# Cutting the last two output tiles of a two-layer MLP by columns, side by side, instead of tile by tile

## The chip, the cores and the metric

The kernel runs on one core of a Trainium2 chip. The metric is the device time of one execution in microseconds. The profile counts from the core's first profiled instruction; its span is about 1.3 us shorter than the timed figure. All timed comparisons below use executions in the fast state, and the granted TensorE clock in them (the share of full speed that the chip allowed) is 1.0. A store's landing is the last of the semaphore updates by which the DMA engines report it done.

## The reference

```python
# x: 2048 x 448, w1: 448 x 1792, w2: 1792 x 448, all bfloat16
h = jnp.einsum("bsd,df->bsf", x, w1) + b1
h = jax.nn.gelu(h, approximate=True)
return jnp.einsum("bsf,fd->bsd", h, w2) + b2
```

## The kernel before

The 2048 rows are worked through in four chunks of 512, that is four output tiles of 128 rows each. Layer 1 leaves gelu(h), transposed, in `g`: 14 blocks of 128 features. Layer 2 contracts over those 14 blocks. Each block is split into its lower and upper 64 rows, and the two halves of the TensorE array work on them side by side. I call them the two lanes. A "unit" is a pair of PSUM banks. In pass "a" the lower lane writes bank 0 and the upper lane bank 1; in pass "b" they swap, so that each bank has seen all 128 rows.

```python
def part(self, name, fts):                      # one pass of a unit
    for ft in fts:                              # 14 feature blocks: 14 "steps"
        for lo in (0, 1):                       # bank
            half = lo if name == "a" else 1 - lo    # lane
            rows = slice(half * H, (half + 1) * H)
            o = 0
            for i, (tile, d0, n) in enumerate(self.banks[lo]):
                # ... one matmul of n columns, with a weight load of its own
                mm(u, lo, half, slice(o, o + n), g[rows, ft, j * P:(j + 1) * P],
                   w2_sb[rows, ft, d0:d0 + n], ...)
                o += n
    # after pass "b": drain. Bank 0 by VectorE (adds b2), in the last chunk's q and r
    # bank 1 by ScalarE (copies; b2 is already in it, by a matmul of ones with b2)
```

The last chunk cannot hide its own drains and stores, so it is cut to leave little for the end. With tile numbers within the chunk, columns from and count (DQ = 112):

```python
p = Layer2(c, [(0, 0, D)], [(1, 0, D)])                          # tiles 0 and 1, 448 columns each
q = Layer2(c, [(2, 0, 3 * DQ)], [(2, 3 * DQ, DQ), (3, 0, 2 * DQ)])
r = Layer2(c, [(3, 2 * DQ, DQ)], [(3, 3 * DQ, DQ)])
p.part("a", every); q.bias(1); r.bias(0); q.part("a", every)
p.part("b", every); r.part("a", every)
q.part("b", every); r.part("b", every)
# ... stores of tiles 0 and 1, then:
store(j + 2, [("o", j + 2, 0), ("o", j + 2, 3 * DQ)])            # SP, 128 rows of 896 bytes
store(j + 3, [("o", j + 3, 0)], 0, 2 * DQ)                       # SP, 128 rows of 448 bytes
store(j + 3, [("o", j + 3, 2 * DQ), ("o", j + 3, 3 * DQ)], 2 * DQ, D, "scalar")
```

## Time and profile before

| | before |
|---|---|
| median time, three runs at first | 93.97 us |
| median time, six runs beside the changed kernel | 94.12 us (93.96 to 94.34) |
| span of the profiled run | 92.8 us |
| matmuls | 969 |
| first bias matmul of the last chunk | 82.263 us |
| start of VectorE's last drain | 90.656 us |
| issue of the last store (ScalarE) | 91.027 us |
| its first packet | 92.007 us |
| its last landing | 92.777 us |

The lower rows are read from the records behind the timeline and the DMA packets, to three decimals. The first bias matmul is a good zero, because everything that the change touches in the last chunk lies after it.

### The profile page before, as it was taken

The numbers are of one execution on the slowest core, as the hardware profiler recorded it, in microseconds if no ns is written. First come the engines' busy times: TensorE is split into PE (matmuls) and PEld (weight loads), VectorE is DVE, ScalarE is ACT, GpSimd is POOL, SyncE is SP. The second block draws the span as 40 slices with busy tenths as digits, with TensorE's granted clock in tenths as the row PEclk, the third lists the DMA queues.
The fourth block names the chain that finished last, engine by engine and source line by source line (L and its number), as shares of the span: only waits on it lengthen the run. The fifth ranks groups of instructions, "written<-read, shape, count | busy, mean of one in ns | idle before, by whom it ended". The sixth has DMA issues, their size and how long they took to land.

```text
span 92.8 us, 2119 instructions
## 1 busy us (share of the span) xinstructions
PE 89.8 (97%) x969; PEld 47.9 (52%) x969; DVE 13.9 (15%) x38; ACT 38.2 (41%) x64; POOL 1.7 (2%) x8
## 2 busy tenths in 40 slices
PE   6999999999999999999999999999999999999990
PEld 2455444555554444555544444555554444579990
DVE  0176000210442000000433000000333000000331
ACT  6033978600004787800003787900002888900021
POOL 6000000000000000000000000000000000000000
PEclk9999999999999999999999999999999999999999
DMA  2999994955747000000033000000022000000023
GB/s 46 342 273 337 375 297 43 207 96 112 70 90 221 14 0 7 0 0 0 0 103 102 0 0 4 0 7 0 0 99 99 7 0 0 0 0 7 0 99 99
DMA packets 12888, 7.32 MB, mean 79 GB/s; under 512 B 7248, under 2 KB 12688, under 8 KB 12880
## 3 DMA queue, kind: packets, MB, share of 16 engines
q1 hardware_dynamic: 11904, 6.75, 31.3%
q10 hardware_dynamic: 944, 0.45, 1.6%
q8 instruction: 7, 0.11, 0.5%
q14 instruction: 1, 0.01, 0.0%
q0 software_dynamic: 32, 0.00, 0.0%
HBM read 3.79 MB, written 1.84 MB: 61 GB/s over the span
## 4 chain that ended last, share of the span: by engine, by line
PE 97%; ACT 0%; issue 0%
PE u L221 92%; PE u L196 4%; PE u L358 1%; ACT out_sb L338 0%
## 5 line engine op out<-in xcount | busy, mean ns | idle before, releaser
L279 ACT ACTIVATE g<-u,b_f 128x512 bf16<-128x512 f32 x56 | 34.8, 685 | 39.5 <-PE u L221 39.5
L221 PE MATMUL u<-w_sb,g 64*128 64x448 bf16 (+3 forms) x532 | 43.3, 320 | 0.0
L221 PE MATMUL u<-xT,w_sb 64*128 64x512 bf16 (+1 forms) x342 | 41.3, 375 | 0.1
L221 PEld LDWEIGHTS u<-w_sb,g 64*128 64x128 bf16 x532 | 25.9, 94 | 16.9
L221 PEld LDWEIGHTS u<-xT,w_sb 64*128 64x128 bf16 x342 | 17.0, 94 | 19.1 <-DVE xT L371 0.3
L341 DVE TENSOR_TENSOR out_sb<-u,b_bc 128x448 bf16<-128x448 f32 (+2 forms) x16 | 8.9, 590 | 62.5 <-PE u L221 62.5
L221 PE MATMUL u<-xT,w1r 64*128 64x512 bf16 x56 | 10.5, 376 | 0.0
L221 PEld LDWEIGHTS u<-xT,w1r 64*128 64x128 bf16 x56 | 2.8, 94 | 3.2
L338 ACT CAST out_sb<-u 128x112 bf16<-128x112 f32 (+1 forms) x3 | 0.8, 286 | 8.8 <-PE u L221 8.8
L196 PE MATMUL u<-const-bfloat16-1.0 128*128 128x512 bf16 (+1 forms) x8 | 3.4, 601 | 0.8 <-PEq L498 0.8
L369 ACT COPY xT<-u 64x256 bf16<-64x256 bf16 (+1 forms) x3 | 1.1, 369 | 3.7 <-PE u L358 2.3
L196 PEld LDWEIGHTS u<-const-bfloat16-1.0 128*128 128x128 bf16 x8 | 1.0, 139 | 2.4 <-issue 2.4
L371 DVE TENSOR_SCALAR xT<-u 128x128 uint32<-128x128 uint32 (+1 forms) x7 | 1.8, 288 | 0.8 <-PE u L358 0.8
L179 ACT ACT_TABLE_LOAD x1 | 1.3, 1283 | 0.8 <-PEq L498 0.8
L449 DVE COPY b_z<-b_bc 1x112 bf16<-1x112 bf16 (+1 forms) x3 | 0.5, 188 | 7.0 <-DMA b_bc<-in_b_dram 6.9
L358 PEld LDWEIGHTS u<-ident,xn 64*128 64x128 bf16 x24 | 0.9, 127 | 0.7 <-issue 0.7
L191 DVE COPY xT<-xT 64x512 bf16<-64x512 bf16 x3 | 0.9, 289 | 2.0 <-DMA xT<-in_x_dram 1.9
L358 PE MATMUL u<-ident,xn 64*128 64x64 bf16 x24 | 1.0, 236 | 0.0
L185 DVE STREAM_TRANSPOSE b1t<-b1n 32x32 bf16<-32x32 bf16 x4 | 0.8, 202 | 0.1
L382 DVE COPY xr<-xn 128x256 bf16<-128x256 bf16 x1 | 0.2, 226 | 3.1 <-DMA xn<-in_x_dram 3.1
L421 DVE COPY w1r<-w1r 64x256 bf16<-64x256 bf16 (+1 forms) x2 | 0.6, 288 | 0.7 <-DMA w1r<-in_w_dram 0.7
L177 POOL DMA_DIRECT2D b1n<-in_b_dram x1 | 0.6, 647 | 0.0
(14 smaller groups left out, 2.8 us busy)
## 6 DMA issues: line engine op xcount, KB each, us to landing
out_dram<-out_sb SPq DMA_DIRECT2D x15, 112.0 KB, 1.7
w_sb<-in_w_dram SPq DMA_DIRECT2D x2, 784.0 KB, 9.2
w_sb<-in_w_dram SPq DMA_DIRECT2D x1, 576.0 KB, 6.2
xn<-in_x_dram SPq DMA_DIRECT2D x1, 448.0 KB, 3.2
w_sb<-in_w_dram ACTq DMA_DIRECT2D x2, 192.0 KB, 4.0
w_sb<-in_w_dram SPq DMA_DIRECT2D x1, 384.0 KB, 5.4
xT<-in_x_dram SPq DMA_TRANSPOSE x12, 4.0
w1r<-in_w_dram SPq DMA_DIRECT2D x1, 160.0 KB, 5.4
```

Source lines behind the costliest of these rows:

```text
L177: pr.dma("gpsimd", lambda e: e.dma_start(b1n[0:NFT, :], b1.rearrange("(c p) -> c p", p=P)), "b1n", after=["b1z"])
L179: pr.op("scalar", lambda e: e.activation(junk[:, :], one, ACT.Gelu_apprx_tanh), event="table")
L185: pr.op("vector", lambda e, q=q: e.transpose(b1t[32 * q:32 * q + 32, :], b1n[:, 32 * q:32 * q + 32]), after=["b1n"], event=("b1t", q))
L191: pr.op("vector", lambda e: e.tensor_copy(xT[0:H, KT, s0:s1], xT[H:P, KT, s0:s1]), after=after, event=event)
L196: pr.op("tensor", lambda e: e.matmul(unit[0][:, 0, 0:cols], lhsT=ones_w, rhs=ones_m[:, 0:cols], start=True, stop=True))
L221: o = pr.op("tensor", lambda e: e.matmul(unit[u][:, lo, cols], lhsT=lhsT, rhs=rhs, start=start, stop=stop, skip_group_check=skip), after=a ...
L279: pr.op("scalar", lambda e, lo=lo, ft=ft: e.activation(g[:, ft, c * SC:(c + 1) * SC], unit[u][:, lo, :], ACT.Gelu_apprx_tanh, bias=b1_f[:, ...
L338: pr.op("scalar", lambda e, j=j, d0=d0, n=n, o=o: e.copy(out_sb[:, j, d0:d0 + n], unit[u][:, 1, o:o + n]), after=[self.done(1)], event=event)
L341: pr.op("vector", lambda e, j=j, d0=d0, n=n, lo=lo, o=o: e.tensor_tensor(out=out_sb[:, j, d0:d0 + n], in0=unit[u][:, lo, o:o + n], in1=b2_ ...
L358: pr.op("tensor", lambda e, half=half, rows=rows: e.transpose(o(half), i(rows), ident[rows, rows]), after=["ident"] + after, event=event i ...
L369: pr.op(engine, lambda e: e.copy(out(BF16), in_(BF16)), after=after, event=event)
L371: pr.op(engine, lambda e: e.tensor_single_scalar(out(U32), in_(U32), 0, ALU.bitwise_or), after=after, event=event)
```

## The change

The intent is to drop the three-matmul steps of q. The same 448 columns per lane are cut as 320 + 128 for both tiles, so every bank is one matmul a step. Since the pieces of tiles 2 and 3 then have equal columns, both leave in one store.

```diff
-    DQ = D // 4
+    DL = D - P
...
+        def store_pair(engine, j, d0, d1, after):
+            pr.dma(engine, lambda e: e.dma_start(
+                out2[j * P:(j + 2) * P, d0:d1].rearrange("(t p) d -> p t d", p=P), out_sb[:, j:j + 2, d0:d1]),
+                "out", after=after)
...
-                q = Layer2(c, [(2, 0, 3 * DQ)], [(2, 3 * DQ, DQ), (3, 0, 2 * DQ)])
-                r = Layer2(c, [(3, 2 * DQ, DQ)], [(3, 3 * DQ, DQ)])
+                q, r = Layer2(c, 2, 0, DL), Layer2(c, 2, DL, D)
...
-                store(j + 2, [("o", j + 2, 0), ("o", j + 2, 3 * DQ)])
-                store(j + 3, [("o", j + 3, 0)], 0, 2 * DQ)
-                store(j + 3, [("o", j + 3, 2 * DQ), ("o", j + 3, 3 * DQ)], 2 * DQ, D, "scalar")
+                for d0, d1, engine in ((0, DL, "sync"), (DL, D, "scalar")):
+                    store_pair(engine, j + 2, d0, d1, [("o", j + 2, d0), ("o", j + 3, d0)])
```

The rest of the diff lets `Layer2` describe one matmul a bank, and prepares the b2 rows in two copies instead of three.

More of the change, by code (lines that the diff above doesn't have):

```diff
@@ L282, in act, with store, __init__ @@
                     busy[(u, lo)] = ("g", c, ft)
-        def store(j, after, d0=0, d1=D, engine="sync"):
-            rows = o0v[:, j, d0:d1] if j < STC else out2[j * P:(j + 1) * P, d0:d1]
-            pr.dma(engine, lambda e: e.dma_start(rows, out_sb[:, j, d0:d1]), "out", after=after)
+        def store(j, after):
+            pr.dma("sync", lambda e: e.dma_start(
+                o0v[:, j, :] if j < STC else out2[j * P:(j + 1) * P, :], out_sb[:, j, :]), "out", after=after)
+        def store_pair(engine, j, d0, d1, after):
+            pr.dma(engine, lambda e: e.dma_start(
+                out2[j * P:(j + 2) * P, d0:d1].rearrange("(t p) d -> p t d", p=P), out_sb[:, j:j + 2, d0:d1]),
+                "out", after=after)
         class Layer2:
-            def __init__(self, c, *banks):
-                self.c, self.banks, self.u = c, banks, next_unit()
+            def __init__(self, c, tile, d0=0, d1=D):
+                self.c, self.tile, self.d0, self.d1, self.u = c, tile, d0, d1, next_unit()
                 self.fresh = [True, True]
@@ L297, in bias @@
                 rows = slice(half * H, (half + 1) * H)
-                n = sum(n for _, _, n in self.banks[1])
-                o = 0
-                for i, (_, _, n) in enumerate(self.banks[1]):
-                    mm(self.u, 1, half, slice(o, o + n), ones_w[rows, :], b2_z[rows, o:o + n], i == 0, False,
-                       free(self.u) + ["b2z"], None, len(self.banks[1]) > 1)
-                    o += n
+                mm(self.u, 1, half, slice(0, self.d1 - self.d0), ones_w[rows, :], b2_z[rows, self.d0:self.d1],
+                   True, False, free(self.u) + ["b2z"])
                 self.fresh[1] = False
@@ L309, in part @@
                     for lo in (0, 1):
+                        j = c * STC + self.tile + lo
                         half = lo if name == "a" else 1 - lo
                         rows = slice(half * H, (half + 1) * H)
-                        o = 0
-                        for i, (tile, d0, n) in enumerate(self.banks[lo]):
-                            j = c * STC + tile
-                            fin = name == "b" and ft == NFT - 1
-                            after = [("g", c, ft), ("w2", ft - ft % 7)] + (free(u) if self.fresh[lo] else [])
-                            mm(u, lo, half, slice(o, o + n), g[rows, ft, j * P:(j + 1) * P], w2_sb[rows, ft, d0:d0 + n],
-                               self.fresh[lo], fin, after, self.done(lo) if fin and i + 1 == len(self.banks[lo]) else None,
-                               len(self.banks[lo]) > 1)
-                            self.fresh[lo] = False
-                            o += n
+                        fin = name == "b" and ft == NFT - 1
@@ L322, in part @@
+                        after = [("g", c, ft), ("w2", ft - ft % 7)] + (free(u) if self.fresh[lo] else [])
+                        mm(u, lo, half, slice(0, self.d1 - self.d0), g[rows, ft, j * P:(j + 1) * P],
+                           w2_sb[rows, ft, self.d0:self.d1], self.fresh[lo], fin, after,
+                           ("y", j, self.d0) if fin else None)
+                        self.fresh[lo] = False
                 if name == "b" and NFT - 1 in fts:
                     self.drain()
-            def done(self, lo):
-                return ("y", self.c, self.banks[0][0], lo)
@@ L328, in drain @@
             def drain(self):
-                u = self.u
-                last = self.c == NSC - 1 and self.banks[1][0][2] < D
+                u, d0, d1 = self.u, self.d0, self.d1
                 for lo in (0, 1):
-                    o = 0
-                    for tile, d0, n in self.banks[lo]:
-                        j = self.c * STC + tile
-                        event = ("o", j, d0)
-                        if last and lo:
-                            pr.op("scalar", lambda e, j=j, d0=d0, n=n, o=o: e.copy(
-                                out_sb[:, j, d0:d0 + n], unit[u][:, 1, o:o + n]), after=[self.done(1)], event=event)
-                        else:
-                            pr.op("vector", lambda e, j=j, d0=d0, n=n, lo=lo, o=o: e.tensor_tensor(
-                                out=out_sb[:, j, d0:d0 + n], in0=unit[u][:, lo, o:o + n], in1=b2_bc[:, d0:d0 + n],
-                                op=ALU.add), after=[self.done(lo), "b2"], event=event)
-                        busy[(u, lo)] = event
-                        o += n
+                    j = self.c * STC + self.tile + lo
+                    if lo and d1 - d0 < D:
+                        pr.op("scalar", lambda e, j=j: e.copy(out_sb[:, j, d0:d1], unit[u][:, 1, 0:d1 - d0]),
+                              after=[("y", j, d0)], event=("o", j, d0))
+                    else:
+                        pr.op("vector", lambda e, j=j, lo=lo: e.tensor_tensor(
+                            out=out_sb[:, j, d0:d1], in0=unit[u][:, lo, 0:d1 - d0], in1=b2_bc[:, d0:d1], op=ALU.add),
+                            after=[("y", j, d0), "b2"], event=("o", j, d0))
+                    busy[(u, lo)] = ("o", j, d0)
@@ L445, in bass_standalone__dense_activation_gelu__prompt_kernel @@
             else:
-                for row, o, d0, n in ((0, 0, 3 * DQ, DQ), (H, 0, 3 * DQ, DQ), (H, DQ, 0, 2 * DQ)):
-                    pr.op("vector", lambda e, row=row, o=o, d0=d0, n=n: e.tensor_copy(
-                        b2_z[row:row + 1, o:o + n], b2_bc[row:row + 1, d0:d0 + n]),
-                        after=["b2", "b2z0"], event="b2z" if o else None)
+                for row in (0, H):
+                    pr.op("vector", lambda e, row=row: e.tensor_copy(b2_z[row:row + 1, :], b2_bc[row:row + 1, :]),
+                          after=["b2", "b2z0"], event="b2z" if row else None)
             if c + 1 < NSC:
@@ L454, in bass_standalone__dense_activation_gelu__prompt_kernel @@
             head, tail, every = range(0, 10), range(10, NFT), range(NFT)
-            p = Layer2(c, [(0, 0, D)], [(1, 0, D)])
+            p = Layer2(c, 0)
             j = c * STC
             if c + 1 < NSC:
-                q = Layer2(c, [(2, 0, D)], [(3, 0, D)])
+                q = Layer2(c, 2)
                 for part in (head, tail):
```

## The prediction

> **What bounds the kernel now.** I read the page of the profile first, then the busy time by stretch over the last few microseconds, then the timeline of the tail, then the DMA issues. The page's engine table and its chain of waits:
>
> ```profile
> PE 89.8 (97%) x969; PEld 47.9 (52%) x969; DVE 13.9 (15%) x38; ACT 38.2 (41%) x64; POOL 1.7 (2%) x8
> ...
> PE 97%; ACT 0%; issue 0%
> PE u L221 92%; PE u L196 4%; PE u L358 1%; ACT out_sb L338 0%
> ```
>
> TensorE is the bound almost from end to end, so only two things in this change can move the time: how long the matmuls of the last two tiles occupy TensorE, and what follows the last matmul. That second part is in the timeline (columns: start, duration, engine, line, operation; the span is 92.8 us):
>
> ```profile
> 89.87 0.75 PE L221 MATMUL u<-w_sb,g 64*128 64x112 bf16 x22
> ...
> 90.01 0.50 ACT L338 CAST out_sb<-u 128x112 bf16<-128x112 f32 x2 [8.64 <-PE u L221]
> 90.50 0.81 SPq L286 DMA_DIRECT2D out_dram<-out_sb  x2
> 90.66 0.28 DVE L341 TENSOR_TENSOR out_sb<-u,b_bc 128x112 bf16<-128x112 f32 x1 [0.18 <-PE u L221]
> 90.69 0.25 ACT L338 CAST out_sb<-u 128x112 bf16<-128x112 f32 x1 [0.18 <-PE u L221]
> 91.03 0.37 ACTq L286 DMA_DIRECT2D out_dram<-out_sb  x1
> ```
>
> Matmuls end at 90.62 (modelled end), the last ScalarE copy at 90.94, its store is issued at 91.03 and lands just before 92.8. About 2.2 us of tail, most of it one store's latency. The two SP stores lie just ahead of it. DMA issues (size, median us to landing), the last three rows being those of this tail:
>
> ```profile
> out_dram<-out_sb SPq DMA_DIRECT2D x15, 112.0 KB, 1.7
> out_dram<-out_sb SPq DMA_DIRECT2D x1, 56.0 KB, 1.7
> out_dram<-out_sb ACTq DMA_DIRECT2D x1, 56.0 KB, 1.8
> ```
>
> Half the bytes don't land sooner: latency is nearly fixed. Busy time by stretch gives the packets (columns end in granted clock, DMA share, GB/s):
>
> ```profile
> 88.70:89.30 0.60, 0.60 (x18) 0.60 (x15) 0.00 (x0) 0.00 (x0) 0.00 (x0) 1.00 0.56 193
> ...
> 91.80:92.00 0.20, 0.00 (x0) 0.00 (x0) 0.00 (x0) 0.00 (x0) 0.00 (x0) 1.00 0.71 195
> 92.00:92.40 0.40, 0.00 (x0) 0.00 (x0) 0.00 (x0) 0.00 (x0) 0.00 (x0) 1.00 0.68 190
> 92.40:92.90 0.50, 0.00 (x0) 0.00 (x0) 0.00 (x0) 0.00 (x0) 0.00 (x0) 1.00 0.00 0
> ```
>
> One 112 KB store (128 rows of 896 bytes, so 8 on each of 16 engines) occupies each engine 0.60 x 0.56 = 0.34 us, 42 ns a row. The two 56 KB stores at the end take 0.2 x 0.71 + 0.4 x 0.68 = 0.41 us for 16 rows of 448 bytes, 26 ns a row. They run back to back: ScalarE's packets begin at 92.01 in the trace, as the first engine finishes SP's second store, so the last store waits a little behind it. After the data ends near 92.40 some 0.39 us pass until the last semaphore update.
>
> **What the Trainium skill says.** "TensorE: Matmul & The Clock Gate", section "Wait — 56ns, not 53.3ns?", gives a warm matmul N / 2.4 GHz plus about 2.5 ns start to start. The trace agrees: in p's second pass each of the two row tiles starts a 448-column matmul every 189 ns (timeline 84.6 to 86.8: 27 matmuls of 349 ns within 2.81 us, so 13 intervals in 2.46 us), in r's a 112-column one every 49 ns (22 of 209 ns in 0.75 us, so 11 intervals in 0.54 us). 140 ns for 336 columns is 2.4 columns a ns, with 2.4 ns left over each. "TensorEngine Tiling (Array Packing)", section "Key Properties", says that different tiles execute weight loads and matmuls in parallel; those two numbers hold for both halves at once, so I count two independent lanes. "DMA: Bandwidth & Descriptors", section "Specifications", names 512 bytes as the smallest transfer for line rate; the 448-byte rows here take 26 ns against 42 ns for 896, so they cost more per byte, with no cliff. Its section "Issuing engines are not separate DMA queues" says that stores from SP and ScalarE end on the same 16 engines and only save issue time; the trace agrees, as above.
>
> **The change part by part.**
>
> *Matmuls.* Before, q holds tile 2 columns 0:336 in one bank and 112 + 224 columns in the other, so three matmuls a step; r holds 112 beside 112. After, q is 320 beside 320 and r 128 beside 128. Columns per lane stay at 448 a step and pass. Removed are 14 matmuls in each pass of q, 28 with their weight loads, 14 in each lane, plus one bias matmul. The lane on the upper rows, which finishes last, had 72 matmuls (2 bias, 28 in q first pass, then 14, 14, 14) and gets 57: 15 x 2.4 = 36 ns, and its bias row has 16 columns fewer, 7 ns. Sum -43 ns. The other lane: 14 x 2.4 = 34 ns less, 16 bias columns more, -27 ns; it ended 90 ns earlier and doesn't matter. So the 28 weight loads of 94 ns, though they look like 2.6 us of work, are worth 0.04 us: they lie beside streaming. The last matmul's result is ready at 90.61 instead of 90.66.
>
> *Drains.* q's DVE drain shrinks from 507 ns (336 columns) to about 490: slope (507 - 276) / 224 = 1.03 ns a column. q's ScalarE copies 252 + 352 ns become one of about 437 (slope 100 ns / 112 columns = 0.89). Both end near 90.32, clear of r's drains. r's drains grow by 16 columns: ScalarE 253 to 267 ns, +14 on the path. So the last store issues at 91.03 - 0.043 + 0.014 = 91.00.
>
> *Stores.* SP had two, issued at 90.50 and 90.88. Now it has one of 160 KB, issued at about 90.35 (both drains done at 90.32, 0.03 to issue as before), first packet 0.84 us after issue as before (90.50 to 91.34), so at 91.19. Its 256 rows of 640 bytes are 16 an engine; between 26 and 42 ns that is 33 ns, 0.52 us, plus 0.13 us between the engines' starts: done near 91.83. ScalarE's store, 0.84 to 0.87 after 91.00, has its first packet near 91.86 in place of 92.01: -0.15, with hardly anything ahead of it. But it now has 256 rows of 256 bytes instead of 128 of 448. On the same line a 256-byte row is 19 ns (an estimate from the two measured sizes), so 16 x 19 = 0.30 us against 8 x 26 = 0.21: +0.09. An issue that describes twice the rows may itself take a little longer; I allow +0.03 (an estimate; the first loads of three blocks took 444 to 512 ns to issue on ScalarE, beside 366 here, with other things going on).
>
> *Elsewhere.* The preparation of the bias rows goes from three VectorE copies to two wider ones; that group costs 0.5 us and waits for a load at 16 us, far from the path. p's drains and stores move some 0.09 us earlier, hidden under q's second pass.
>
> Sum: -0.03 (to the issue) - 0.15 + 0.09 + 0.03 = -0.06 us. Predicted 93.97 - 0.06 = 93.91, that is 93.9 us.
>
> **Rivals.** (1) *Small rows bite.* The 256-byte rows could cost as much each as the 448-byte ones, or more: per-row cost 26 ns gives 16 x 26 = 0.42 us, +0.12 more than above, and a doubled descriptor count could lengthen the start by another 0.2. Then 94.0 to 94.25. For it: 26 against 42 ns shows a fixed share in each row. Against: from 896 to 448 bytes the row cost still fell by 16 ns. (2) *The bigger SP store collides.* If its start is late or its rows slow, the last store queues behind 160 KB instead of 56 KB; each 0.1 us of delay goes to the end. Both drains it waits for end before 90.35, so I expect at most 0.1: 94.0. (3) *Weight loads were the bound in the narrow stretches.* The weight-load row is busy all of 87 to 90 us, against 0.84 in the 448-column pass, and 28 loads of 94 ns over two lanes are 1.3 us: 92.7. Against it, the 49 ns pace at 112 columns follows the same 2.4 columns a ns law as 448 columns; a load-bound stretch would be slower than that. I give this 3 in 100. Even this would be 1.4%, under the 2% line.
>
> **Range and chances.** The terms are all tenths of a microsecond; 2% would be 1.9 us. The three timed runs before spread over 0.29 us. With rival 1 above and a little more saved in the tail below, 93.65 to 94.2 should hold it 8 times in 10. Faster by over 2%: 0.01; within 2%: 0.98; slower: 0.01.
>
> **What would show each step.** 969 - 28 - 1 = 940 matmuls on TensorE; starts every 136 ns in q and 56 ns in r per lane, last drain starting at 90.61 for VectorE; ScalarE's last copy 267 ns, its store issued at 91.00; SP's one late store issued near 90.35; packets of ScalarE's store from 91.86 to about 92.3; span 92.75. Wrong would be: a pace in r above 56 ns, SP's pair issued after 90.5, a gap over 1.0 us between ScalarE's issue and its first packet, or its landing over 1.9 us, which would point to rival 1.

## The result

The changed kernel took 93.92 us (median of six, 93.72 to 94.13) beside 94.12 us for the kernel before. The ratio is 0.9979, with a 95% interval from 0.9956 to 1.0003: the same within 2%, and not told apart from 1. The page of the profile after:

```profile
PE 89.3 (96%) x940; PEld 46.9 (51%) x940; DVE 13.9 (15%) x37; ACT 38.2 (41%) x63; POOL 1.7 (2%) x8
...
PE 86%; DMA 7%; SPq 2%; ACT 1%; ACTq 1%; issue 1%
```

29 matmuls are gone, as counted. The chain of waits now names DMA with 7%, which it did not before. That is a load of weights at 4.0 to 10.5 us of the chain, not in what was changed: the busy time by stretch shows where the two profiled runs part. First before, then after (columns: stretch, length, TensorE busy, weight loads, VectorE, ScalarE, GpSimd, clock, DMA share, GB/s):

```profile
0.00:16.00 16.00, 15.17 (x140) 7.26 (x142) 3.67 (x16) 9.32 (x16) 1.70 (x8) 1.00 1.05 246
16.00:82.00 66.00, 66.00 (x660) 32.75 (x656) 8.29 (x18) 28.09 (x46) 0.00 (x0) 1.00 0.19 44
```

```profile
0.00:16.00 16.00, 14.89 (x142) 6.94 (x144) 4.17 (x18) 9.51 (x17) 1.71 (x8) 1.00 0.97 262
16.00:82.00 66.00, 66.00 (x660) 31.95 (x658) 7.81 (x15) 27.95 (x45) 0.00 (x0) 1.00 0.19 40
```

From 16 to 82 us TensorE has no idle time in either. In all fourteen traces, from the first layer-2 matmul of the first chunk to the first bias matmul of the last chunk it is 66.15 or 66.16 us. But that first layer-2 matmul comes anywhere from 15.68 to 16.58 us, kernel by kernel and run by run. This scatter of 0.9 us is ten times what the change moves, so I compare stretches that start at the first bias matmul. Where they begin, before and after, in the timeline of TensorE:

```profile
82.26 0.30 PE L221 MATMUL u<-b_z,const-bfloat16-1.0 64*128 64x112 bf16 x3
```

```profile
82.08 0.30 PE L221 MATMUL u<-b_z,const-bfloat16-1.0 64*128 64x128 bf16 x2
```

And the end, after, from the timeline (start, duration, engine, line, operation), the DMA issues, and the busy time by stretch:

```profile
89.69 0.43 ACT L329 CAST out_sb<-u 128x320 bf16<-128x320 f32 x1 [8.49 <-PE u L221]
89.85 0.55 PE L221 MATMUL u<-w_sb,g 64*128 64x128 bf16 x12
...
90.20 0.38 SPq L289 DMA_DIRECT2D out_dram<-out_sb  x1
90.43 0.29 DVE L332 TENSOR_TENSOR out_sb<-u,b_bc 128x128 bf16<-128x128 f32 x1 [0.29 <-PE u L221]
90.47 0.27 ACT L329 CAST out_sb<-u 128x128 bf16<-128x128 f32 x1 [0.35 <-PE u L221]
90.82 0.39 ACTq L289 DMA_DIRECT2D out_dram<-out_sb  x1
```

```profile
out_dram<-out_sb SPq DMA_DIRECT2D x1, 160.0 KB, 2.0
out_dram<-out_sb ACTq DMA_DIRECT2D x1, 64.0 KB, 1.7
```

```profile
91.30:91.75 0.45, 0.00 (x0) 0.00 (x0) 0.00 (x0) 0.00 (x0) 0.00 (x0) 1.00 0.86 246
91.75:91.80 0.05, 0.00 (x0) 0.00 (x0) 0.00 (x0) 0.00 (x0) 0.00 (x0) 1.00 0.45 110
91.80:92.15 0.35, 0.00 (x0) 0.00 (x0) 0.00 (x0) 0.00 (x0) 0.00 (x0) 1.00 0.75 174
92.15:92.50 0.35, 0.00 (x0) 0.00 (x0) 0.00 (x0) 0.00 (x0) 0.00 (x0) 1.00 0.00 0
```

By the packet records SP's big store leaves the first engine at 91.61 and the last by 91.80, and ScalarE's begins at 91.76, in the stretch of share 0.45: they only touch. Before, two stores stood back to back there. Matmuls of 128 columns end at 90.40 (89.85 + 0.55), 8.3 us after the bias.

Stage by stage, in us:

| stage | before | after | difference |
|---|---|---|---|
| first bias matmul to last drain (VectorE start) | 8.393 | 8.352 | -0.041 |
| last drain to issue of the last store | 0.371 | 0.384 | +0.013 |
| issue to its first packet | 0.980 | 0.940 | -0.040 |
| first packet to last landing | 0.770 | 0.754 | -0.016 |
| landing to end | 0.034 | 0.034 | 0 |
| sum | 10.548 | 10.464 | -0.084 |

### The profile page after: what moved, and what is told of

Same layout as the page of the kernel before. It is cut to its first block, busy times and chain, and to the rows that moved or that the text cites. A ratio compares the mean times of both kernels' runs of the same rounds, so it can differ in the third digit from the quotient of the medians.

```text
span 92.5 us, 2058 instructions
## 1 busy us (share of the span) xinstructions
PE 89.3 (96%) x940; PEld 46.9 (51%) x940; DVE 13.9 (15%) x37; ACT 38.2 (41%) x63; POOL 1.7 (2%) x8
## 4 chain that ended last, share of the span: by engine, by line
PE 86%; DMA 7%; SPq 2%; ACT 1%; ACTq 1%; issue 1%
PE u L221 86%; DMA w_sb<-in_w_dram 7%; SPq L141 1%; SPq L134 1%; ACTq L134 1%; ACT L179 1%; ACT out_sb L329 0%; ACT junk L179 0%
## 5 line engine op out<-in xcount | busy, mean ns | idle before, releaser
L221 PE MATMUL u<-w_sb,g 64*128 64x448 bf16 (+2 forms) x504 | 43.2, 328 | 0.0
L221 PE MATMUL u<-xT,w1r 64*128 64x512 bf16 x56 | 10.5, 376 | 0.0
L329 ACT CAST out_sb<-u 128x320 bf16<-128x320 f32 (+1 forms) x2 | 0.7, 346 | 8.8 <-PE u L221 8.8
L438 DVE COPY b_z<-b_bc 1x448 bf16<-1x448 bf16 x2 | 0.5, 267 | 6.6 <-DMA b_bc<-in_b_dram 6.6
```

The lines of the kernel that those rows point to most:

```text
L221: o = pr.op("tensor", lambda e: e.matmul(unit[u][:, lo, cols], lhsT=lhsT, rhs=rhs, start=start, stop=stop, skip_group_check=skip), after=a ...
```

## The experiments

Theory: the 29 matmuls are worth 2.4 ns each on their lane and nothing for their weight loads; the store is worth what it no longer waits, less what its doubled rows cost. Rivals: weight loads bound the narrow stretches; the rows or the bigger SP store eat the gain. e1, e4, e5, e6 and e12 are single looks, with one run and an unknown state; I take from them only stretches in the trace, at a clock of 1.0. Runs e5, e9 and e10 edit the kernel before, the others the changed kernel.

### e12_before_again: how steady are the stages?

No edit.

> The kernel before, profiled once more, to see how far the stages of one trace can be trusted. The changed kernel's stretch from the first bias matmul to the end came as 10.464 and 10.465 us in two traces on separate occasions. If the tail of the kernel before is as steady, it is 10.53 to 10.57 us again, with 8.39 us of it to the last drain and 1.74 to 1.76 us from the last issue to the last landing; the first bias matmul itself may lie anywhere from 81.8 to 82.8 us.

Measured: 10.550 us from bias to end, 8.393 to the last drain, 1.753 from issue to landing, with the first bias matmul at 82.698. Beside 10.548, 8.393 and 1.750 this shows the stages steady to about 3 ns while their start moved by 0.4 us. Differences of 0.02 us in a stage can be read.

### e11_after_again: the changed kernel timed again

No edit.

> The changed kernel unchanged, timed again in five rounds. From the stages of the traces, the change is worth 0.08 to 0.09 us from the first bias matmul to the end (10.46 us against 10.55), so a ratio of 0.999; the first measurement gave 0.9979 with an interval from 0.9956 to 1.0003. If the larger gain of 0.2 us were real, the second measurement would have its interval below 1 again around 0.998; if the rest was scatter of the first 16 us, where these runs differ by up to 0.7 us, the ratio comes anywhere from 0.996 to 1.003, and the traced stretch again at 10.46 us.

Measured: median 94.05 us, ratio 0.9992 with an interval from 0.9959 to 1.0026, and 10.465 us in the trace. The stretch repeats; the timed gain of 0.2 us does not. The 0.084 us of the trace would be a ratio of 0.9991 (0.084 over 94), which both timings allow and neither proves.

### e1_third_mm: the matmul part undone

```diff
-                        mm(u, lo, half, slice(0, self.d1 - self.d0), ...)
+                        cuts = (0, 96, 320) if lo and self.d0 == 0 and self.d1 == DL else (0, self.d1 - self.d0)
+                        for a, b in zip(cuts, cuts[1:]):
+                            mm(u, lo, half, slice(a, b), ...)     # and the bias matmul likewise
```

> Only the matmul part of the change is undone: q's second bank is again two matmuls a step, of 96 and 224 columns (and two bias matmuls), in the layout, drains and stores of the changed kernel. I measure from the first bias matmul to the start of VectorE's last drain: 8.39 us before the change, 8.35 after it. If each extra matmul costs 2.4 ns on its lane and its weight load nothing (my theory), the lane on the upper rows gets 15 of them, +36 ns, so 8.39 us; the tail after it stays as in the changed kernel. If weight loads were the bound there (rival), each of the 28 would cost up to 94 ns on its lane, +1.3 us, so 9.7 us.

Measured, with the start and the end of the stretch in the timeline:

```profile
82.31 0.30 PE L221 MATMUL u<-b_z,const-bfloat16-1.0 64*128 64x96 bf16 x3
90.69 0.29 DVE L336 TENSOR_TENSOR out_sb<-u,b_bc 128x128 bf16<-128x128 f32 x1 [0.29 <-PE u L221]
```

That is 8.386 us in the records, +34 ns over the changed kernel, and issue to landing is 1.701 us as in it. So 36 ns was right. Twenty-eight more matmuls and weight loads (and one bias matmul) cost 34 ns, not 1.3 us. The other 7 of the change's 41 ns are what 16 fewer bias columns on the upper lane come to; that is a sum, not a run.

### e2_quarters: the suspected cost multiplied

```diff
-                        mm(u, lo, half, slice(0, self.d1 - self.d0), ...)
+                        cuts = (0, 80, 160, 240, 320) if self.d0 == 0 and self.d1 == DL else (0, self.d1 - self.d0)
+                        for a, b in zip(cuts, cuts[1:]):
+                            mm(u, lo, half, slice(a, b), ...)     # and the bias matmul likewise
```

> The suspected cost is multiplied: both banks of q are four matmuls of 80 columns a step instead of one of 320, so each lane gets 84 more matmuls and weight loads over q's two passes, and the upper lane 3 more bias matmuls. If the law N / 2.4 + 2.4 ns still holds at 80 columns (35.7 ns), the stretch from the first bias matmul to the last drain grows by 87 x 2.4 = 0.21 us, to 8.56 us. If the weight loads become the bound below some width, it grows by more: at a floor of 47 ns a matmul and lane (half of a load's 94 ns) by 28 x (4 x 47 - 135.7) = 1.5 us, to 9.8 us, and the kernel becomes 1.5% slower.

Measured: ratio 1.0058 to the kernel before (1.0029 to 1.0086), median 94.62 us. Its timeline at the start and the end of the stretch:

```profile
82.47 0.23 PE L221 MATMUL u<-b_z,const-bfloat16-1.0 64*128 64x80 bf16 x3
```

```profile
91.03 0.29 DVE L336 TENSOR_TENSOR out_sb<-u,b_bc 128x128 bf16<-128x128 f32 x1 [0.29 <-PE u L221]
```

91.03 - 82.47 = 8.56 us (8.566 in the records), as the law N / 2.4 + 2.4 ns has it. At 80 columns a matmul and lane, 36 ns, the weight loads still hide. In this trace the loads come in pairs every 36 ns, one for each lane, though each is recorded as 97 ns long: the recorded length of a load is not the time for which its lane is taken. The third rival of the prediction has fallen: a narrow matmul costs its fixed 2.4 ns and no more here.

### e10_uneven: are the lanes really independent?

```diff
-                q = Layer2(c, [(2, 0, 3 * DQ)], [(2, 3 * DQ, DQ), (3, 0, 2 * DQ)])
-                r = Layer2(c, [(3, 2 * DQ, DQ)], [(3, 3 * DQ, DQ)])
+                q = Layer2(c, [(2, 0, D)], [(3, 0, 192)])
+                r = Layer2(c, [(3, 192, 128)], [(3, 320, 128)])
```

> Tests that the two row halves are independent lanes, beside offering one more layout without a third matmul: q is tile 2 whole (448 columns) beside tile 3's first 192, r is tile 3's last 128 + 128; over q's two passes each lane has the same number of columns, but within a pass one lane has 448 and the other 192 a step. If lanes run freely ahead of each other, the stretch from the first bias matmul to the last drain stays at 8.35 us (plus or minus 0.05). If a lane cannot run far ahead[...], each step of q takes as long as 448 columns, 189 ns, in both passes: 28 x (189 - 136) = 1.5 us more, 9.85 us, and the kernel is 1.5% slower than the changed one.

Measured: 9.629 us to the last drain, ratio 1.0135 (1.0097 to 1.0174), median 95.33 us. The groups of matmuls between 83.3 and 84.5 us, in q's first pass:

```profile
L221 PE MATMUL u<-w_sb,g 64*128 64x448 bf16 x8 | 1.7, 349 | 0.0
L221 PE MATMUL u<-w_sb,g 64*128 64x192 bf16 x8 | 1.5, 252 | 0.0
```

The stretch is 0.22 us short of the 9.85 expected, but far from 8.35. Eight of each: the 192-column lane goes at the pace of the 448-column one, 189 ns a step, where it would need 82. It first ran ahead, then stood in step some three matmuls ahead, at its fourteenth as the other reached its eleventh. So here the lanes overlapped but did not drift far. The prediction's "independent" holds only for equal columns in each step, which both kernels have. Why the lead stops at about three is not settled by this run.

### e4_alone_after and e5_alone_before: the last store with nothing ahead of it

Their outputs are wrong, which doesn't matter for the times. The first leaves SP's pair out of the changed kernel, the second SP's two late stores out of the kernel before:

```diff
-                for d0, d1, engine in ((0, DL, "sync"), (DL, D, "scalar")):
-                    store_pair(engine, j + 2, d0, d1, ...)
+                store_pair("scalar", j + 2, DL, D, ...)
```

```diff
-                store(j + 2, [("o", j + 2, 0), ("o", j + 2, 3 * DQ)])
-                store(j + 3, [("o", j + 3, 0)], 0, 2 * DQ)
```

> A wrong result on purpose: SP's late pair of stores (columns 0 to 320) is left out of the changed kernel, so ScalarE's last store runs alone on the DMA engines. In the changed kernel its first packet came 0.94 us after its issue and its last landing 1.69 us after it. If SP's 160 KB were in its way, the first packet now comes at about 0.84 us, as for SP's stores, and the landing at about 1.59. If 0.94 is its own latency, nothing changes.

> A wrong result on purpose: the kernel before, without SP's two late stores, so ScalarE's store of 128 rows of 448 bytes runs alone. In the kernel before its first packet came 0.98 us after its issue, as SP's second store left the first engine, and its last landing 1.75 us after it. My prediction took the difference to SP's 0.84 us as queueing. If so, the first packet now comes at 0.84 to 0.88 us and the landing at about 1.62. If ScalarE's store has that latency by itself, first packet 0.98 and landing 1.75 stay.

The DMA issues of ScalarE's queue (size, us to landing), first of the changed kernel without the pair, then of the kernel before without its SP stores:

```profile
out_dram<-out_sb ACTq DMA_DIRECT2D x1, 64.0 KB, 1.7
```

```profile
out_dram<-out_sb ACTq DMA_DIRECT2D x1, 56.0 KB, 1.6
```

The second was 1.8 in the page before; the first has not moved. To three decimals, from the records:

| issue of the last store to | first packet | last landing |
|---|---|---|
| before, behind SP's stores | 0.980 | 1.750 |
| before, alone (e5) | 0.874 | 1.580 |
| changed, with SP's pair | 0.940 | 1.694 |
| changed, alone (e4) | 0.913 | 1.694 |

These four rows settle the store. In the kernel before, SP's two late stores cost the last one 0.17 us (1.750 - 1.580): 0.106 before its first packet and 0.064 in the spread of its packets. That the second of them, which the packet records show directly ahead, did it alone is not shown, since e5 takes out both. In the changed kernel SP's pair costs 0.027 us at the first packet and nothing at the landing. Alone against alone, 256 rows of 256 bytes land 0.114 us later than 128 rows of 448: 0.04 us of it before the first packet (the issue itself takes 394 ns instead of 366), the rest in 16 packets of 17.1 ns an engine instead of 8 of 23.7. Net -0.17 + 0.11 = -0.06 us.

### e3_singles: the pairing undone

```diff
-                for d0, d1, engine in ((0, DL, "sync"), (DL, D, "scalar")):
-                    store_pair(engine, j + 2, d0, d1, [("o", j + 2, d0), ("o", j + 3, d0)])
+                for t, d0, d1, engine in ((2, 0, DL, "sync"), (3, 0, DL, "sync"), (2, DL, D, "sync"), (3, DL, D, "scalar")):
+                    store_one(engine, j + t, d0, d1, [("o", j + t, d0)])
```

> Only the pairing of stores is undone: the columns and drains of the changed kernel, but each tile's piece leaves in a store of its own, three by SP (320, 320, then tile 2's last 128 columns) and tile 3's last 128 columns by ScalarE. The last store is then 128 rows of 256 bytes instead of 256. If the packets of the last store are what its tail is made of, issue to last landing falls from 1.69 us to about 1.69 - 8 x 0.017 = 1.55 us. If SP's store issued just before it gets in its way on the same DMA engines, as the second SP store did in the kernel before, the tail stays at 1.65 to 1.75 us and pairing is neutral. In time, 93.8 to 94.0 either way, within 0.2% of the changed kernel.

Measured: ratio 1.0023 (0.9996 to 1.0050), median 94.16 us, above the 93.8 to 94.0 expected, and 10.578 us from bias to end, 0.114 us more than with pairs. The last issues in the timeline:

```profile
91.19 0.91 SPq L289 DMA_DIRECT2D out_dram<-out_sb  x2
91.41 0.37 ACTq L289 DMA_DIRECT2D out_dram<-out_sb  x1
```

Neither expectation had what happened: SP was still busy issuing its second store, so its third went out at 91.67, 0.26 us after ScalarE's at 91.41, and landed last, although quickly (1.607 us). Pairing saves the sequencer's time: one issue of 383 ns instead of 332 + 432.

### e7_pair_then_singles: the pair kept first, undone last

```diff
+                store_pair("sync", j + 2, 0, DL, [("o", j + 2, 0), ("o", j + 3, 0)])
+                for t, engine in ((2, "sync"), (3, "scalar")):
+                    store_one(engine, j + t, DL, D, [("o", j + t, DL)])
```

> The pair stays for the first 320 columns, where it saves SP an issue, and is undone for the last 128 columns: tile 2's piece by SP and tile 3's by ScalarE, each 128 rows of 256 bytes, issued side by side. With singles throughout, SP's third store was issued at 0.26 us after ScalarE's since SP was busy with its second, and landed 1.61 us after issue against 1.69 for the pair. If the rows of the last store are what costs, and SP is free in time now, both land 1.6 to 1.65 us after issues within 0.08 us of each other: end 0.03 to 0.08 us earlier than the changed kernel, measured from the first bias matmul (10.46 us), so 10.38 to 10.43. If two issues at once hold each other up (SP's took 432 ns instead of 332 beside ScalarE's), 10.46 or more.

Measured: 10.428 us from bias to end, 0.036 us less than the changed kernel, at the upper end of what was expected. ScalarE's store, issued at 90.512, waited for SP's of 90.501: first packet 0.998 us after issue, landing 1.719. The timed ratio, 1.0011 (0.9980 to 1.0043), tells nothing. It is the shortest end of a kernel with a right result that I found, and not shown faster by the timed runs.

### e6_sp_last: the last pair from SP

```diff
-                for d0, d1, engine in ((0, DL, "sync"), (DL, D, "scalar")):
+                for d0, d1, engine in ((0, DL, "sync"), (DL, D, "sync")):
```

> The changed kernel with the last pair issued by SP, as its first pair is, instead of ScalarE. SP's first pair had its first packet 0.90 us after issue, ScalarE's 0.94. If the queue makes no difference and only the doubled rows cost, first packet at 0.90 to 0.94 us and landing at 1.65 to 1.70 us after issue; the issue itself may come 0.03 us sooner after the last drain, since ScalarE spends 0.085 us between its copy's end and its issue.

Measured: first packet 0.913 us and landing 1.695 us after issue, end at 10.450 us. The issue came 0.072 us after ScalarE's copy ended, against 0.085. The queue makes no difference worth having.

### e8_r64: the cut at 384 and 64 columns

```diff
-    DL = D - P
+    DL = D - 64
```

> The changed kernel with the cut at 384 and 64 columns instead of 320 and 128. ScalarE's last copy falls by 64 x 0.89 = 57 ns; the last store has 128-byte rows, about 12 ns each by the line through 17, 34 and 42 ns, so its 16 rows an engine take 0.08 us less. If the matmul law holds at 64 columns (29 ns a lane) the stretch from the first bias matmul to the last drain stays at 8.35 us less 64 bias columns (27 ns) on the upper lane plus the same added, so 8.35 to 8.38, and the end comes 0.1 to 0.15 us earlier, at 10.32 to 10.36 us after the bias. If weight loads become the bound below 80 columns, at a floor of 36 ns a matmul, r's two passes lose 28 x 7 = 0.2 us and the end comes later, at 10.5 us or more.

Measured: ratio 1.0052 (1.0025 to 1.0078), median 94.37 us, end at 10.811 us, later by 0.35 us. Its two issues in the timeline, and the DMA share (last but one column) by stretch:

```profile
90.84 0.38 SPq L289 DMA_DIRECT2D out_dram<-out_sb  x1
90.98 0.40 ACTq L289 DMA_DIRECT2D out_dram<-out_sb  x1
```

```profile
91.70:92.50 0.80, 0.00 (x0) 0.00 (x0) 0.00 (x0) 0.00 (x0) 0.00 (x0) 1.00 0.85 265
92.50:92.70 0.20, 0.00 (x0) 0.00 (x0) 0.00 (x0) 0.00 (x0) 0.00 (x0) 1.00 0.57 87
```

The expected loss, by weight loads, did not come: r's matmuls of 64 columns still start every 29 ns a lane. The loss is the collision, the prediction's second rival. r's second pass is now so short (14 x 29 = 0.4 us) that q's wide drain is still running at its end. SP's 192 KB store goes out only 0.14 us ahead of ScalarE's, whose first packet comes 1.35 us after issue, at 92.33, as the first engine leaves SP's store at 92.32; the engines are 0.85 busy with SP's alone until then. VectorE's last drain also starts some 0.07 us late, behind its q drain. So 128 columns for r is not about matmul width; it is the time that q's drain and store need.

### e9_pool_store: the kernel before, with GpSimd issuing the middle store

```diff
-                store(j + 3, [("o", j + 3, 0)], 0, 2 * DQ)
+                store(j + 3, [("o", j + 3, 0)], 0, 2 * DQ, "gpsimd")     # on a semaphore of its own
```

> A possible version better than both: the kernel before, with SP's second late store (tile 3, columns 0 to 224) issued by GpSimd instead, on its own semaphore, in parallel with SP's first. With no SP stores at all the end came 10.375 us after the first bias matmul; with both it was 10.55, with the changed kernel 10.46. If GpSimd's packets come within 1.3 us of its issue at about 90.5 us on the before-trace's scale, they clear the engines before ScalarE's (issue 91.03, first packet 0.87 us later), and the end comes at 10.38 to 10.43. If GpSimd's issue is slower than that, they collide and the end is at 10.5 or later; its one other DMA took 0.65 us to issue.

Measured: 10.684 us from bias to end, ratio 1.0022 (0.9978 to 1.0066). GpSimd issued at 90.80, some 0.3 us after its data was ready, its first packet came 1.15 us later, and ScalarE's store waited until 92.12. The end is where the second expectation had it. What came late was the issue itself, not the 1.15 us after it, which is under the 1.3 us allowed.

## Why the prediction was right

The predicted -0.06 us and the traced -0.084 us are both far inside 2%. That 93.91 us came so near the measured 93.92 us is luck, since the first 16 us scatter by 0.9 us and the kernel before was itself timed 0.15 us slower beside it. The -0.06 us is in part luck too, because the sum counts one term twice. Its "-0.15" compares positions in the trace, 91.86 in place of 92.01, and 91.86 already starts from the earlier issue at 91.00; so "-0.03 (to the issue)" is in it. The wait alone is 0.86 in place of 0.98, -0.12, and the prediction's own terms add up to -0.03.

*Matmuls.* Right: -43 ns predicted, -41 measured between the bias and the last drain, and e1 and e2 give the same law when it is undone or multiplied.

*Drains.* Right: +14 ns predicted on the path, +13 measured. ScalarE's copy took 266 ns, VectorE's q drain 492, ScalarE's 426.

*Stores.* Right in mechanism, mis-sized in the wait. The last store waited behind SP's stores and no longer does, and its doubled rows give part of that back. By the prediction's own figures the wait was 0.12 us, all before the first packet; e5 against the kernel before gives 0.106 there and 0.17 at the landing. The 0.03 us counted twice makes up for most of this lack of 0.05. "+0.09" and "+0.03" for the doubled rows was 0.114 by e4 against e5. The step that failed is the first packet "0.84 to 0.87" us after issue, 0.89 with the 0.03 allowed: it was 0.940, and 0.913 even alone. I had used the latency of a 128-row store for one of 256 rows; SP's own pair shows the same, 0.904 instead of 0.836. So the first packet gained 0.040 us where 0.09 was predicted, and the stretch from there to the landing became 0.016 us shorter instead of 0.09 longer. SP's pair was issued, on the scale of the profile before, at 90.38 (90.201 plus the 0.181 by which the bias came sooner), near the 90.35 predicted, and left the last engine at 91.98 instead of 91.83.

*Rivals.* Rival 1 cost less than feared: 17.1 ns a row, below the 19 estimated. Rival 2 cost 0.027 us at the first packet and nothing at the landing, but e8 shows that it lies close by. Rival 3 is refuted by e1 and e2.

*Elsewhere.* No sign that the copies of b2 reached the path: they run at 15.01 to 15.56 us, when VectorE had been idle for 6.6 us and has nothing else to do before 18 us, and the 66.15 us from the first chunk's layer 2 to the bias is the same.

What stays open: what sets the scatter of the first 16 us. The chain of waits names loads of w1 there in three of the fourteen traces, all of the changed kernel or a variant of it (after, e11, e6), and not in the others; no experiment here tested it.

## What to carry to other kernels

Removing matmuls that only split a fixed number of columns saves the fixed cost of each, here 2.4 ns, even where weight loads look busy all the time. Keep the lanes' columns equal in each step. At the end of a kernel, count the stores that precede the last one and the rows it is made of: queueing behind two others cost the last store 0.17 us here, and twice as many rows gave 0.11 of that back. When run-to-run scatter is ten times the effect, choose a zero in the trace after the scatter and compare stretches.

## What the Trainium skill lacked or had wrong

- "TensorEngine Tiling (Array Packing)", section "Key Properties", has tiles operate independently, and that section gives no limit. In e10_uneven the matmuls of the narrower lane started up to three steps ahead of program order, and the lane was then held to the other's 189 ns a step; 1.28 us were lost against the changed kernel.
- "TensorE: Matmul & The Clock Gate", section "Back-to-back issue gap", gives about 81 ns a matmul at 128 columns for streams with a weight load each. Here, with row tiles, it was 56 ns a lane, and 36 ns at 80 and 29 ns at 64 columns, each with its weight load: the law of the section "Wait — 56ns, not 53.3ns?" held instead.
- "DMA: Bandwidth & Descriptors", section "Specifications", gives a first-byte latency of about 0.6 us for SP and ScalarE, and a line-rate limit of 512 bytes. From issue to first packet it was 0.84 us (SP) and 0.87 us (ScalarE) with 128 rows, and 0.90 to 0.91 us with 256; that section has no term for the number of rows and does not say where it starts to count. From the end of the issue's record it was 0.50 to 0.52 us in all four. Rows of 128, 256, 448, 512, 640 and 896 bytes took 12.5, 17, 24, 26, 34 and 42 ns, with no step at 512.
